# Second-stage expert products over 408 instead of 416 slots, in an order planned anew

## The chip, the cores and the metric

The kernel runs on one core of a Trainium2 chip. The metric is the time of one execution on the device in microseconds (us); less is better. Engines are named as in the profile: PE is TensorE's matmul, PEld its weight load, DVE is VectorE, ACT is ScalarE, POOL is GpSimd and SP is SyncE, which here only issues DMAs.

## The reference, cut to what matters

Three layers follow each other on 1536 tokens of 512 numbers. The first is attention in which a query sees only keys of the same hash bucket. The second is a mixture of 8 experts in which each token goes to one expert. The third is the one that the change touches most: each token goes to the two best of 8 experts.

```python
def _moe2_ref(x, w_gate, w_noise, noise, w1, w2):
    logits = x @ w_gate
    noisy_logits = logits + np.log1p(np.exp(x @ w_noise)) * noise
    top2 = np.argpartition(-noisy_logits, 2, axis=1)[:, :2]
    ...
    for e in range(E):
        for k in range(2):
            mask = top2[:, k] == e
            h = np.maximum(x[mask] @ w1[e], 0.0)
            out[mask] += top2_w[mask, k, None] * (h @ w2[e])
```

On the drawn inputs the second mixture sends 386, 404, 368, 376, 389, 374, 397 and 378 tokens to its experts (counted from the reference).

## The kernel before

**Stages.** Attention and the routing of the first mixture are one planned phase. Both mixtures together are the second phase. In it an expert is called a key: keys 0 to 7 are the first mixture's experts, keys 8 to 15 the second's. A token's row is scattered to its expert's slots in DRAM (`xs1`, `xs2`), and an expert's rows are read back from there. An expert of the second mixture has `CAP2` = 416 slots; a token beyond that is counted by `run_over`, and a count over zero runs a slow fallback over all tokens.

**One expert.** `x_turn`, `x_h` and `x_l` turn its rows and split each number into a high and a low half in a reduced float type. `mm1` forms the first product in four pairs of pieces, `relu_h` and `relu_l` apply the ReLU and split again, `mm2` forms the second product in eight pieces (blocks d = 0 to 3, halves p = 0 and 1). A piece is 12 matmuls: three products (high-high, low-high, high-low) for each 128 rows of the contraction. The moving operand has one column for each slot, so its width is `cap`. Weights come in chunks of 512 KB, eight for an expert, issued by SP into a ring of four raw buffers; ACT copies the high half (`wsplit_h`) and DVE subtracts the low one (`wsplit_l`).

**After the product.** For keys 8 to 14, ACT copies a finished block from PSUM to `YS` (`y_copy`), DVE turns it in 32 x 32 blocks (`y2_turn`, 13 blocks of 32 slots, so it reads all 416 columns) and weights it (`y2_weight`), and POOL adds it to the output in 13 scatters (`y2_add`). There is one buffer `yo` for the turned rows, so a key's first turn waits until the scatters of the key before have landed. Key 15 is different: its rows are gathered from the output (`y2_gather`), added on chip, and written by four scatters (`y2_put`), in four blocks of `MB` = 104 slots. Three blocks go through `mm2` (312 columns) and transposes, the fourth is formed row by row in two halves (`mm2_rows`, 256 columns). Key 8 is special at its start: part of its rows is read back in four blocks of `MB` rows and transposed by PE, and `y_put` adds the rows of the last first-mixture expert straight into PSUM.

**What sets the order.** Every engine works its instructions in the order in which they were emitted. A planner (`Plan.order`) decides that before the kernel is built. Each step has an engine, an assumed length in ns, the steps that it needs, the buffers that it holds, and a due time in us. The planner goes through time with these lengths. At each choice it takes, among the steps that could start within a short look-ahead (`WAITS`, `WAITS2`: a fixed time or a share of the step's length), the one with the earliest due time. `LENGTH` and `LENGTH2` replace assumed lengths by others; a pair is a length and a landing delay after it. `SHIFT` and `SHIFT2` add to the due times of groups of steps. In the second phase a group is a step's kind and a letter: a for keys 0 to 5, b for 6 to 8, c for 9 to 14, d for 15. `m1` and `m2` are the pieces of the two products, with due times `z + 2.1 * (2 * fp + f)` and `z + 2.1 * (8 + 2 * d + p)` for keys 8 to 15, where z is 37 us later for each key. The step `wr` stands for a weight chunk's transfer.

Of the kernel before, what the change touches and what calls it, by code (L numbers as in the profile page):

```python
# [13 lines left out]
AF = mybir.ActivationFunctionType  # L14
# [7 lines left out]
N, D, E, F = NB * S, NHEAD * DH, 8, 1024  # L22
NT = N // 128
CAP1 = 224
PB = CAP1 // 2
CAP2 = 416
MB = CAP2 // 4
NQ = CAP2 // 32
RW1 = D + 2 + E
RW2 = D + 1 + E  # L30
# [28 lines left out]
WAITS = {'PE': (0, 0.0), 'ACT': (95, 0.2), 'DVE': (35, 0.53), 'POOL': (1120, 0.0)}  # L59
LENGTH2 = {('POOL', 'gm', 1742): 2363, ('POOL', 'iw', 1100): 750, ('ACT', 'wh', 520): 521, ('DVE', 'wl', 600): 602, ('Q', 'wr', 2100): (2100, 1500), ('POOL', 'xm', 1023): 783,  # L60
    ('ACT', 'xh', 241): 243, ('DVE', 'xlo', 303): 310, ('ACT', 'xh', 427): 470, ('DVE', 'xlo', 536): 533, ('PE', 'm1', 1336): 1340, ('ACT', 'rh', 425): 441,
# [5 lines left out]
    ('DVE', 'xm', 150): 105, ('PE', 'xt', 430): 224, ('ACT', 'xh', 400): 403, ('DVE', 'xlo', 503): 509, ('ACT', 'xh', 745): 791, ('DVE', 'xlo', 936): 933,  # L67
# [3 lines left out]
SHIFT2 = {'g1a': -170, 'g2a': -15, 'g2b6': -95, 'g4a': -35, 'g5a': 1.3, 'g5aa': -230, 'g8a': -15, 'g9a': 26, 'gia': 23,  # L71
    'gib6': -120, 'gpa': -15, 'm1a': -13, 'm1b': 16, 'm1d': 5, 'm2a': -8, 'm2b': 19, 'm2c': 8, 'rha': -45,
    'rhb': -170, 'rla': -25, 'rlb': 60, 'rlc': -65, 'rld': -65, 'sqa': -17, 'wh0a': -20, 'wh1a': -15, 'wh1b': -115,
    'wl0a': -33, 'wl0b': 60, 'wl0c': 35, 'wl0d': -120, 'wl1a': -18, 'wl1b': 78, 'wl1c': 20, 'wl1d': -60, 'wr0a': -15,
    'wr0b': -20, 'wr1a': -30, 'wr1b': -35, 'xla': -20, 'xlb': -125, 'xloa': -120, 'xlob': -85, 'xloc': 75, 'xmc': 50,
    'xmd': -120, 'xta': -20, 'xtc': -40, 'yc0b': -55, 'yca': -10, 'yra': -5, 'yta': -2, 'ywd': -15}
WAITS2 = {'PE': (120, 0.0), 'ACT': (120, 0.5), 'DVE': (0, 0.01), 'POOL': (120, 0.0)}
WAIT = 120
ROUTING = ("rsa", "rsb", "r7", "rm", "rr0", "rr", "rq", "rp", "rn", "rv", "re", "rg", "ra", "rc", "ro", "xa", "xb", "oh", "xo")
PR = dict(sc=-5.4, mx=-8.7, ex=-5.34, pv=3.37, fin=3.38, bits=-14.64, prep=-18.57, load=-37.69, h=-17.66, l=0)  # L80
# [11 lines left out]
LATE, ZP, Z2, L6, CR = 1, 21.9, 205.0, -4, 12  # L92
# [88 lines left out]
def lsh_attention_moe_moe2_kernel(  # L181
# [144 lines left out]
    def run_over(pool, pi, i8, cap, K, T, dst, va=None, n=128):  # L326

        g = nc.gpsimd
        p = pool.tile([n, 2, K, T], F32, name="ov")
        g.tensor_copy(p[:, 0], pi)  # L330
        g.tensor_copy(p[:, 1], i8[:, :, 0:K].rearrange("p t k -> p k t"))
        g.tensor_scalar(p[:, 1], p[:, 1], float(N), float(cap), op0=OP.mult, op1=OP.add)
        g.tensor_tensor(p[:, 0], p[:, 0], p[:, 1], op=OP.subtract)
        if va is None:
            g.tensor_scalar(dst, p[:, 0], 0.0, None, op0=OP.is_ge)
        else:
            g.tensor_scalar(p[:, 1], p[:, 0], 0.0, None, op0=OP.is_ge)
            g.tensor_tensor(dst, p[:, 1], va[:, None, :].to_broadcast([n, K, T]), op=OP.mult)
# [854 lines left out]
    def y_copy(key, cap, d):  # L1193
        YS[key, d] = yp.tile([128, CAP2], F32, name="ys", bufs=6)
        o = cap if halves(key, d) else 0
        nc.scalar.activation(YS[key, d][:, :cap], Y[key, d][:, o:o + cap], AF.Copy)

    def y_add(key, cap, d):
        nc.vector.tensor_tensor(YS[key, d][:, :cap], Y[key, d][:, :cap], YS[key, d][:, :cap], op=OP.add)
# [65 lines left out]
    def y_put(dp, b):  # L1265
        for k in range(2):
            for d in range(2):
                x = ROWS[b, dp][k][:, d * 128:d * 128 + 128]
                nc.tensor.matmul(XP[E, 2 * dp + d][:, :CAP2], x, ONES[0][:, b], start=False, stop=b + k == 2)

    def r2_rank0(e):
        R2[e]["R"] = psp.tile([128, 512], F32, name="O", bufs=1)
# [14 lines left out]
        scat2.append(s)  # L1287

    def r2_over(e):
        run_over(r2, R2[e]["pi"], R2[e]["i8"], CAP2, 2, 2,  # L1290
                 rmax[:PB, NT + 4 * e:NT + 4 * e + 4].rearrange("p (k t) -> p k t", k=2), VA[e], PB)


# [12 lines left out]
    def x2_load(e):  # L1306
        if e:
            x2_rest(e)
            X2[e] = x_load(xs2, e, CAP2)
        else:  # L1310
            X2[0] = xin.tile([128, 4 * D], F32, name="xr")[:, :4 * D].rearrange("p (b c) -> p b c", c=D)
            nc.sync.dma_start(X2[0][:MB], xs2[0:CAP2].rearrange("(b p) c -> p b c", p=MB)[:, :, :D])

    def x2_rest(e):
        x = XM[8 + e] = yp.tile([128, NQ, RW2 - D], F32, name="xm2", bufs=3)
        if e < E - 1:
            for a in range(4):
                nc.sync.dma_start(x[32 * a:32 * a + 32], xs2[e * N:e * N + CAP2].rearrange("(b j) c -> j b c", j=32)[:, :, D:])
        else:
            nc.sync.dma_start(x[:MB, :4], xs2[e * N:e * N + CAP2].rearrange("(b p) c -> p b c", p=MB)[:, :, D:])  # L1320

    def x2_meta(e):
        if e < E - 1:
# [104 lines left out]
            add(("wl", n, k), "DVE", 600, P(wsplit_l, n, 2, k), z + k + .5, [("wh", n, k)] + ([("xlo", 0, 2)] if (n, k) == (4, 0) else []),  # L1428
                use=([("raw", n)] if n >= 8 else []) + [("w%d" % (c // 4), n)])
    for key in range(2 * E):  # L1430
        z, cap, one = Z[key], CAP1 if key < E else CAP2, key < E
        e = key % E
        q = 1.236 if one else 2.1
        if one:
# [32 lines left out]
        for fp in range(4):  # L1467
            for f in range(2):
                o = z + q * (2 * fp + f)
                add(("m1", key, fp, f), "PE", 1336 if one else 2276, P(mm1, key, cap, fp, f), o,  # L1470
                    [("xlo", key, i) for i in range(1 if fp + f == 0 else len(xp))]
                    + [("wl", key * 8 + fp, 0 if fp + f == 0 else 1)] * (key > 0)
                    + ([("m1", key, fp, 0)] if f else []),
                    use=[("w0", key * 8 + fp)] + [("x", (key, i)) for i in range(len(xp))]
                    + ([("S", ("m", key, fp))] if f else []), new=[] if f else [("S", ("m", key, fp))])
            o = z + q * (2 * fp + 2)
            add(("rh", key, fp), "ACT", 425 if one else 745, P(relu_h, key, cap, fp), o - CR, [("m1", key, fp, 1)],
                use=[("S", ("m", key, fp))], new=[("hh", (key, fp))])
            add(("rl", key, fp), "DVE", 535 if one else 936, P(relu_l, key, cap, fp), o - CR, [("rh", key, fp)],
                use=[("S", ("m", key, fp)), ("hh", (key, fp))])  # L1480
        yk = lambda d: ("S", "y72") if (key, d) == (E - 1, 2) else ("ET", ("y", key, d))
        for d in range(4):
            for p in range(2):
                o = z + q * (8 + 2 * d + p)
                c2 = 3 * MB if key == 2 * E - 1 else cap
                add(("m2", key, d, p), "PE", 1258 if one else 12 * int(c2 * .452 + 2), P(mm2, key, c2, d, p), o,
                    [("rl", key, 2 * p), ("rl", key, 2 * p + 1)]
                    + [("wl", key * 8 + 4 + d // 2 * 2 + p, 1)]
                    + ([("m2", key, d, 0)] if p else []),
                    use=[("w1", key * 8 + 4 + d // 2 * 2 + p)]  # L1490
                    + [("hh", (key, c)) for c in range(2 * p, 2 * p + 2)] + ([yk(d)] if p else []),
                    new=[] if p else [yk(d)])
            o = z + q * (10 + 2 * d)
            add(("yc0" if halves(key, d) else "yc", key, d), "ACT", 238 if one else 398, P(y_copy, key, c2, d), o - CR, [("m2", key, d, 1)],
                use=[yk(d)], new=[("ys", (key, d))])
            if halves(key, d):
                add(("yc", key, d), "DVE", 300, P(y_add, key, c2, d), o - CR, [("yc0", key, d)], use=[yk(d), ("ys", (key, d))])
# [225 lines left out]
```

## Time and profile before

| | us |
|---|---|
| median of 3 runs | 765.57 |
| lowest, highest | 765.16, 767.86 |
| the profiled execution's own time | 765.78 |
| its span, first to last instruction | 764.0 |
| TensorE busy in the span | 748.8 |
| VectorE, ScalarE, GpSimd busy | 569.5, 471.1, 390.8 |

The profiled execution is 1.78 us longer than its span and 0.2 us over the median. Attention fills the first 260 us or so, the first mixture lasts until about 460 us, and the second until 756 us, when TensorE's last matmul begins. A matmul's duration in the trace is longer than the distance to the next one's start, since they are pipelined; what a matmul costs in a row of them is read from the starts.

### The profile page before, as it was taken

To read this page: it belongs to the slowest core of one execution; us is meant where nothing else is said; L and a number is where in the kernel's file an instruction comes from. 1 tells how busy PE (TensorE), PEld (TensorE's weight loads), DVE (VectorE), ACT (ScalarE), POOL (GpSimd) and SP (SyncE) were. 2 spreads that over 40 slices of the span, in tenths; PEclk is the share of its full clock that TensorE was granted. 3 is DMA by queue.
4 is the path that set the end of the run, shared out by engine and by line. 5 is a ranking of instruction groups with operands and counts; after the bars stand their busy time and mean duration, and the time that the engine had idled before them with its cause. 6 is when DMAs were issued, how large, how long until landed. Compare 5 with 4: busy or idle time off the path is not lost. (4 is left out here: it accounts for less than half of the span.)

```text
span 764.0 us, 14517 instructions
## 1 busy us (share of the span) xinstructions
PE 748.8 (98%) x4851; PEld 726.9 (95%) x4851; DVE 569.5 (75%) x1249; ACT 471.1 (62%) x1009; POOL 390.8 (51%) x666
## 2 busy tenths in 40 slices
PE   8999999999999999999999999999999999999995
PEld 7999999999989999999999989999999999999995
DVE  7989989999989858988888766675757575754411
ACT  7889899898878747656566646453445344444210
POOL 6543445566666530445334443028564664748574
PEclk9999999999999999999999999999999999999999
DMA  7778886987774478777678586949797694946143
GB/s 193 190 202 229 213 221 176 274 212 184 161 186 147 151 199 266 215 236 251 194 212 253 178 238 173 222 149 239 142 222 172 137 225 104 218 120 121 18 36 84
DMA packets 142114, 140.61 MB, mean 184 GB/s; under 512 B 25898, under 2 KB 122434, under 8 KB 142034
## 3 DMA queue, kind: packets, MB, share of 16 engines
q1 hardware_dynamic: 124770, 122.93, 58.5%
q0 software_dynamic: 17264, 16.69, 11.5%
q8 instruction: 40, 0.66, 0.4%
q14 instruction: 40, 0.33, 0.1%
HBM read 88.54 MB, written 34.46 MB: 161 GB/s over the span
## 5 line engine op out<-in xcount | busy, mean ns | idle before, releaser
L1359 POOL DMA_INDIRECT out_dram<-yo,idx x91 | 149.6, 1644 | 125.0 <-DVE yo L1356 99.3
L1136 PE MATMUL S<-xh,w0h 128*128 128x224 f32 (+1 forms) x512 | 162.2, 317 | 0.5 <-DVE hh L1149 0.4
L1138 PE MATMUL S<-xh,w0l 128*128 128x224 f32 (+1 forms) x512 | 160.5, 313 | 0.0
L1137 PE MATMUL S<-xl,w0h 128*128 128x224 f32 (+1 forms) x512 | 159.8, 312 | 0.0
L273 DVE TENSOR_TENSOR w1l<-wraw,w1h 128x512 fp32r<-128x512 f32 x128 | 82.8, 684 | 35.9 <-ACT w1h L267 35.6
L693 DVE TENSOR_TENSOR el<-ET,eh 128x384 fp32r<-128x384 f32 x192 | 99.0, 549 | 6.4 <-ACT eh L687 4.9
L1145 ACT ACTIVATE hh<-S 128x448 fp32r<-128x448 f32 (+1 forms) x64 | 45.0, 703 | 93.8 <-PE S L1138 92.2
L687 ACT ACTIVATE eh<-ET 128x384 fp32r<-128x384 f32 x192 | 91.0, 496 | 16.9 <-PE ET L683 16.4
L675 ACT ACTIVATE es<-S,mxs 128x768 f32<-128x768 f32 x96 | 95.9, 999 | 8.2 <-POOL mxs L671 6.2
L665 DVE TENSOR_REDUCE mxs<-S 128x1 f32<-128x768 f32 x96 | 91.6, 954 | 12.3 <-PE S L660 9.3
L1137 PEld LDWEIGHTS S<-xl,w0h 128*128 128x128 f32 x512 | 97.1, 190 | 1.4 <-DVE xl L1122 0.5
L1136 PEld LDWEIGHTS S<-xh,w0h 128*128 128x128 f32 x512 | 97.1, 190 | 1.1 <-DVE hh L1149 0.6
L1138 PEld LDWEIGHTS S<-xh,w0l 128*128 128x128 f32 x512 | 97.2, 190 | 0.4
L267 ACT ACTIVATE w1h<-wraw 128x512 fp32r<-128x512 f32 x128 | 73.2, 624 | 34.6 <-PE ET L1172 27.1
L1149 DVE SCALAR_TENSOR_TENSOR hh<-S,hh 128x448 fp32r<-128x448 f32 (+1 forms) x64 | 52.5, 820 | 52.7 <-ACT hh L1145 52.5
L1172 PE MATMUL ET<-hh,w1h 128*128 128x416 f32 (+2 forms) x264 | 90.2, 342 | 1.1 <-DVE hh L1149 1.1
L1173 PE MATMUL ET<-hh,w1l 128*128 128x416 f32 (+2 forms) x264 | 91.0, 345 | 0.0
L683 PE MATMUL ET<-idf,es 128*128 128x128 f32 x576 | 90.0, 274 | 1.0 <-DVE el L693 1.0
L1171 PE MATMUL ET<-hh,w1h 128*128 128x416 f32 (+2 forms) x264 | 90.4, 343 | 0.0
L267 ACT ACTIVATE w0h<-wraw 128x512 fp32r<-128x512 f32 (+1 forms) x152 | 78.1, 560 | 8.2 <-DMA wraw<-in_w1b_dram 7.1
L273 DVE TENSOR_TENSOR w0l<-wraw,w0h 128x512 fp32r<-128x512 f32 x120 | 77.4, 685 | 7.7 <-ACT w0h L267 7.6
L683 PEld LDWEIGHTS ET<-idf,es 128*128 128x128 f32 x576 | 71.0, 142 | 8.8 <-DVE el L693 1.5
(270 smaller groups left out, 1605.5 us busy)
## 6 DMA issues: line engine op xcount, KB each, us to landing
wraw<-in_w1a_dram SPq DMA_DIRECT2D x32, 512.0 KB, 5.4
wraw<-in_w2a_dram SPq DMA_DIRECT2D x32, 512.0 KB, 4.9
wraw<-in_w1b_dram SPq DMA_DIRECT2D x32, 512.0 KB, 4.4
wraw<-in_w2b_dram SPq DMA_DIRECT2D x32, 512.0 KB, 4.3
xs<-zrow SPq DMA_DIRECT2D x26, 260.5 KB, 4.1
xr<-xs SPq DMA_DIRECT2D x28, 208.0 KB, 4.9
qk<-in_qk_dram SPq DMA_DIRECT2D x15, 384.0 KB, 4.1
xs<-zrow SPq DMA_DIRECT2D x14, 261.0 KB, 3.8
```

The source lines that it names most:

```text
L267: nc.scalar.activation(wH[n][:, c], wraw[n][:, c], AF.Copy)
L273: eng.tensor_tensor(wL[n][:, c], wraw[n][:, c], wH[n][:, c], op=OP.subtract)
L665: nc.vector.tensor_reduce(MX[(3 * g + j) % 9][:, 0:1], SC[g, j][:, :, :384], axis=AX.XY, op=OP.max, negate=True)
L675: nc.scalar.activation(ES[g, j].rearrange("p (a b) -> p a b", a=2), SC[g, j][:, :, :384], AF.Exp, bias=mx[:, 2:3], scale=mx[:, 1:2], accum ...
L683: nc.tensor.transpose(T[:, j * 128:j * 128 + 128], ES[g, j][:, kb * 128:kb * 128 + 128], idf)
L687: nc.scalar.activation(EH[g, kb], ET[g, kb], AF.Copy)
L693: nc.vector.tensor_tensor(EL[g, kb], ET[g, kb], EH[g, kb], op=OP.subtract)
L1136: nc.tensor.matmul(o, wH[n][:, fs], xh, start=kd == 0, stop=False)
L1137: nc.tensor.matmul(o, wH[n][:, fs], xl, start=False, stop=False)
L1138: nc.tensor.matmul(o, wL[n][:, fs], xh, start=False, stop=kd == 3)
L1173: nc.tensor.matmul(P, wL[n][:, ws], hh, start=False, stop=f == 7)
L1359: s = nc.gpsimd.indirect_dma_start(out=out.rearrange("n (a c) -> (n a) c", a=4), out_offset=bass.IndirectOffsetOnAxis(ap=IDX[e][:, b:b + 1 ...
```

## The change

The products of keys 8 to 15 use 408 columns instead of 416. `MB` becomes 102, so key 15's three blocks have 306 columns, and key 8's blocks have 102 rows. Reads of whole experts from `xs2` stay at 416 rows. Since DVE still turns 416 columns of `YS`, one more ACT instruction for each block of keys 8 to 14 fills the last 8 with ones. The overflow count uses 408. In the planner, the override for `wr` is gone, so a weight chunk's landing delay is the step's own 1300 ns instead of 1500. The assumed lengths of the products follow the width, the copy with the filler is longer, and the shifts and look-aheads of the second phase are all other numbers; a look-ahead of the first phase changes in its third digit. So the order of the second phase's instructions changes on every engine.

```diff
+USE2 = 408
-MB = CAP2 // 4
+MB = USE2 // 4
...
-WAITS = {'PE': (0, 0.0), 'ACT': (95, 0.2), 'DVE': (35, 0.53), 'POOL': (1120, 0.0)}
+WAITS = {'PE': (0, 0), 'ACT': (95, 0.2), 'DVE': (35, 0.5337189177802887), 'POOL': (1120, 0)}
...
-LENGTH2 = {('POOL', 'gm', 1742): 2363, ('POOL', 'iw', 1100): 750, ('ACT', 'wh', 520): 521, ('DVE', 'wl', 600): 602, ('Q', 'wr', 2100): (2100, 1500), ('POOL', 'xm', 1023): 783,
+LENGTH2 = {('POOL', 'gm', 1742): 2363, ('POOL', 'iw', 1100): 750, ('ACT', 'wh', 520): 521, ('DVE', 'wl', 600): 602, ('POOL', 'xm', 1023): 783, ('ACT', 'xh', 241): 243,
...
-    ('PE', 'm1', 2276): 2267, ('ACT', 'rh', 745): 761, ('DVE', 'rl', 936): 941, ('PE', 'm2', 2280): 2267, ('ACT', 'yc', 398): 414, ('DVE', 'yt', 502): 528,
+    ('PE', 'm1', 2232): 2222,
+    ('ACT', 'rh', 745): 761, ('DVE', 'rl', 936): 941, ('PE', 'm2', 2232): 2222, ('ACT', 'yc', 598): 640, ('DVE', 'yt', 502): 528, ('DVE', 'yw', 730): 743,
...
-SHIFT2 = {'g1a': -170, 'g2a': -15, 'g2b6': -95, 'g4a': -35, 'g5a': 1.3, 'g5aa': -230, 'g8a': -15, 'g9a': 26, 'gia': 23,
-    'gib6': -120, 'gpa': -15, 'm1a': -13, 'm1b': 16, 'm1d': 5, 'm2a': -8, 'm2b': 19, 'm2c': 8, 'rha': -45,
...
+SHIFT2 = {'g1a': -220, 'g2a': -90, 'g2b6': -90, 'g3a': -80, 'g5a': -10, 'g5aa': -255, 'g8a': 2, 'g9a': 20, 'gca': -100,
+    'gia': 15, 'm1a': -6.7, 'm1b': 15, 'm1c': 18, 'm1d': 25, 'm2a': -10, 'm2b': 15, 'm2c': 25, 'm2d': 140,
...
-WAITS2 = {'PE': (120, 0.0), 'ACT': (120, 0.5), 'DVE': (0, 0.01), 'POOL': (120, 0.0)}
+WAITS2 = {'PE': (85, 0), 'ACT': (120, 0.8), 'DVE': (120, 0), 'POOL': (775, 0)}
...
         nc.scalar.activation(YS[key, d][:, :cap], Y[key, d][:, o:o + cap], AF.Copy)
+        if E <= key < 2 * E - 1:
+            nc.scalar.activation(YS[key, d][:, cap:], ones[:, :CAP2 - cap], AF.Copy)
...
-                nc.tensor.matmul(XP[E, 2 * dp + d][:, :CAP2], x, ONES[0][:, b], start=False, stop=b + k == 2)
+                nc.tensor.matmul(XP[E, 2 * dp + d][:, :USE2], x, ONES[0][:, b, :USE2], start=False, stop=b + k == 2)
...
-        run_over(r2, R2[e]["pi"], R2[e]["i8"], CAP2, 2, 2,
+        run_over(r2, R2[e]["pi"], R2[e]["i8"], USE2, 2, 2,
...
-            nc.sync.dma_start(X2[0][:MB], xs2[0:CAP2].rearrange("(b p) c -> p b c", p=MB)[:, :, :D])
+            nc.sync.dma_start(X2[0][:MB], xs2[0:USE2].rearrange("(b p) c -> p b c", p=MB)[:, :, :D])
...
-        z, cap, one = Z[key], CAP1 if key < E else CAP2, key < E
+        z, cap, one = Z[key], CAP1 if key < E else USE2, key < E
```

## Rows read from the trace of the kernel before

**Rows 1.** The page's first part: span; busy us, share and count of TensorE.

```profile
span 764.0 us, 14517 instructions
PE 748.8 (98%) x4851; PEld 726.9 (95%) x4851; DVE 569.5 (75%) x1249; ACT 471.1 (62%) x1009; POOL 390.8 (51%) x666
```

**Rows 2.** Waits of PE, 430 to 764 us: total us, times, longest.

```profile
PE ET L1172 <- DVE hh L1149: 1.1, 1, 1.1
PE S L807 <- DMA xr<-xs: 0.6, 1, 0.6
PE ET L1220 <- ACT ys L1196: 0.4, 1, 0.4
```

**Rows 3.** Stretches: length; busy PE, PEld, DVE, ACT, POOL; PEclk; DMA share; GB/s.

```profile
480.00:500.00 20.00, 18.92 (x101) 18.39 (x100) 13.65 (x24) 8.03 (x14) 0.00 (x0) 1.00 0.98 243
500.00:520.00 20.00, 20.00 (x108) 19.82 (x107) 16.81 (x26) 12.77 (x22) 7.51 (x4) 1.00 0.54 157
```

**Rows 4.** Timeline of PE, 699 to 752 us: start, duration, line, tiles, shape.

```profile
699.12 0.35 PE L1171 MATMUL ET<-hh,w1h 128*128 128x416 f32 x1
...
716.68 0.35 PE L1171 MATMUL ET<-hh,w1h 128*128 128x416 f32 x1
...
737.12 0.30 PE L1171 MATMUL ET<-hh,w1h 128*128 128x312 f32 x1
...
748.58 0.30 PE L1171 MATMUL ET<-hh,w1h 128*128 128x312 f32 x1
...
749.00 0.28 PE L1183 MATMUL ET<-w1h,hh 128*104 128x256 f32 x1
...
751.48 0.28 PE L1183 MATMUL ET<-w1h,hh 128*104 128x256 f32 x1
```

**Rows 5.** Timeline of POOL, 719 to 764 us; in brackets idle before and its end.

```profile
719.75 1.75 POOL L1359 DMA_INDIRECT out_dram<-yo,idx  x1 [6.32 <-DVE yo L1356]
...
742.20 1.55 POOL L1359 DMA_INDIRECT out_dram<-yo,idx  x1 [0.30 <-issue]
...
757.80 1.00 POOL L1369 DMA_INDIRECT out_dram<-yo,idx  x1 [0.30 <-issue]
```

**Rows 6.** Timeline of DVE, 714 to 757 us.

```profile
714.79 1.60 DVE L1351 STREAM_TRANSPOSE yo<-ys 128x416 f32<-128x416 f32 x3 [4.04 <-DMA out_dram<-yo,idx]
...
718.00 0.61 DVE L1351 STREAM_TRANSPOSE yo<-ys 128x416 f32<-128x416 f32 x1 [0.44 <-ACT ys L1196]
...
738.21 1.02 DVE L1149 SCALAR_TENSOR_TENSOR hh<-S,hh 128x832 fp32r<-128x832 f32 x1 [5.25 <-ACT hh L1145]
752.11 0.48 DVE L1190 SCALAR_TENSOR_TENSOR yo<-ET,wc,xr 104x256 f32<-104x256 f32 x1 [12.87 <-DMA xr<-out_dram,idx]
...
756.18 0.48 DVE L1190 SCALAR_TENSOR_TENSOR yo<-ET,wc,xr 104x256 f32<-104x256 f32 x1 [0.24 <-PE ET L1185]
```

**Rows 7.** Groups of PE by line and shape, whole span: count; busy, mean ns.

```profile
L1136 PE MATMUL S<-xh,w0h 128*128 128x416 f32 x256 | 89.8, 351 | 0.0
L1171 PE MATMUL ET<-hh,w1h 128*128 128x416 f32 x224 | 78.5, 350 | 0.0
```

**Rows 8.** Groups of ACT by line and shape, 440 to 764 us.

```profile
L1145 ACT ACTIVATE hh<-S 128x832 fp32r<-128x832 f32 x32 | 27.7, 866 | 68.3 <-PE S L1138 67.9 <-PE ET L1173 0.3
...
L384 ACT ACTIVATE sp<-lg 112x16 f32<-112x16 f32 x1 | 0.2, 216 | 0.4 <-DVE lg L1241 0.4
```

**Rows 9.** Timeline of PE, 567 to 573 us: starts of pieces at key 10's end.

```profile
567.71 0.35 PE L1136 MATMUL S<-xh,w0h 128*128 128x416 f32 x1
...
569.97 0.35 PE L1171 MATMUL ET<-hh,w1h 128*128 128x416 f32 x1
...
572.24 0.35 PE L1136 MATMUL S<-xh,w0h 128*128 128x416 f32 x1
```

**Rows 10.** Waits of ACT, 480 to 764 us: total us, times, longest.

```profile
ACT w0h L267 <- DMA wraw<-in_w1b_dram: 7.1, 2, 3.6
```

**Rows 11.** Line L1171: weight loads, duration min/median/max in ns, all three widths.

```profile
L1171 PEld LDWEIGHTS ET<-hh,w1h x264: 187/188/192, 448.1 to 748.4; 128*128 128x128 f32 x132
```

More of the change, by code (lines that the diff above doesn't have):

```diff
@@ L58 @@
     'xb6': 60}
-WAITS = {'PE': (0, 0.0), 'ACT': (95, 0.2), 'DVE': (35, 0.53), 'POOL': (1120, 0.0)}
-LENGTH2 = {('POOL', 'gm', 1742): 2363, ('POOL', 'iw', 1100): 750, ('ACT', 'wh', 520): 521, ('DVE', 'wl', 600): 602, ('Q', 'wr', 2100): (2100, 1500), ('POOL', 'xm', 1023): 783,
-    ('ACT', 'xh', 241): 243, ('DVE', 'xlo', 303): 310, ('ACT', 'xh', 427): 470, ('DVE', 'xlo', 536): 533, ('PE', 'm1', 1336): 1340, ('ACT', 'rh', 425): 441,
[5 rows of a table removed]
-    ('DVE', 'xm', 150): 105, ('PE', 'xt', 430): 224, ('ACT', 'xh', 400): 403, ('DVE', 'xlo', 503): 509, ('ACT', 'xh', 745): 791, ('DVE', 'xlo', 936): 933,
[3 rows of a table removed]
@@ L71 @@
-SHIFT2 = {'g1a': -170, 'g2a': -15, 'g2b6': -95, 'g4a': -35, 'g5a': 1.3, 'g5aa': -230, 'g8a': -15, 'g9a': 26, 'gia': 23,
-    'gib6': -120, 'gpa': -15, 'm1a': -13, 'm1b': 16, 'm1d': 5, 'm2a': -8, 'm2b': 19, 'm2c': 8, 'rha': -45,
[L73 to L76, printed above, removed]
@@ L77 @@
-WAITS2 = {'PE': (120, 0.0), 'ACT': (120, 0.5), 'DVE': (0, 0.01), 'POOL': (120, 0.0)}
+WAITS = {'PE': (0, 0), 'ACT': (95, 0.2), 'DVE': (35, 0.5337189177802887), 'POOL': (1120, 0)}
+LENGTH2 = {('POOL', 'gm', 1742): 2363, ('POOL', 'iw', 1100): 750, ('ACT', 'wh', 520): 521, ('DVE', 'wl', 600): 602, ('POOL', 'xm', 1023): 783, ('ACT', 'xh', 241): 243,
[10 rows of a table added]
+SHIFT2 = {'g1a': -220, 'g2a': -90, 'g2b6': -90, 'g3a': -80, 'g5a': -10, 'g5aa': -255, 'g8a': 2, 'g9a': 20, 'gca': -100,
+    'gia': 15, 'm1a': -6.7, 'm1b': 15, 'm1c': 18, 'm1d': 25, 'm2a': -10, 'm2b': 15, 'm2c': 25, 'm2d': 140,
+    'rha': -15, 'rhb': -160, 'rhc': -40, 'rhd': -120, 'rla': -20, 'rlb': 45, 'sqa': -17, 'wh0a': -29, 'wh0b': -31,
+    'wh1a': -22.1, 'wh1b': -110, 'wl0a': -45, 'wl0b': 55, 'wl0d': -85, 'wl1a': -12, 'wl1b': 65, 'wl1c': 30, 'wr0a': -25,
+    'wr0b': -20, 'wr1a': -130, 'wr1b': -70, 'wr1c': 170, 'xha': -35, 'xhb': -15, 'xhc': 80, 'xla': -20, 'xlb': -165,
+    'xloa': -40, 'xloc': 80, 'xtb': 50, 'xtc': -15, 'yc0a': -195, 'yca': -40, 'ycc': 50, 'yra': -19, 'yta': -1}
@@ L1319, in x2_rest @@
         else:
-            nc.sync.dma_start(x[:MB, :4], xs2[e * N:e * N + CAP2].rearrange("(b p) c -> p b c", p=MB)[:, :, D:])
+            nc.sync.dma_start(x[:MB, :4], xs2[e * N:e * N + USE2].rearrange("(b p) c -> p b c", p=MB)[:, :, D:])
     def x2_meta(e):
@@ L1469, in lsh_attention_moe_moe2_kernel @@
                 o = z + q * (2 * fp + f)
-                add(("m1", key, fp, f), "PE", 1336 if one else 2276, P(mm1, key, cap, fp, f), o,
+                add(("m1", key, fp, f), "PE", 1336 if one else 2232, P(mm1, key, cap, fp, f), o,
                     [("xlo", key, i) for i in range(1 if fp + f == 0 else len(xp))]
@@ L1493, in lsh_attention_moe_moe2_kernel @@
             o = z + q * (10 + 2 * d)
-            add(("yc0" if halves(key, d) else "yc", key, d), "ACT", 238 if one else 398, P(y_copy, key, c2, d), o - CR, [("m2", key, d, 1)],
+            add(("yc0" if halves(key, d) else "yc", key, d), "ACT", 238 if one else 398 if key == 2 * E - 1 else 598, P(y_copy, key, c2, d), o - CR, [("m2", key, d, 1)],
                 use=[yk(d)], new=[("ys", (key, d))])
```

14 rows, old and new, of the table LENGTH2 are left out of this document.

## Prediction

> **What bounds the kernel now.** I read the page's first part first: TensorE is busy for 748.8 of 764.0 us and no other engine comes near it [rows 1]. A busy TensorE can still hide waits, so the next view is who TensorE waited for from 430 us on, where the second stage lies: three waits, 1.1 + 0.6 + 0.4 = 2.1 us [rows 2]. By stretches, 480 to 500 us lacks 1.08 us (18.92 of 20), and the twelve stretches from 500 to 740 us all show 20.00 of 20 (the first stands), at a granted clock of 1.00, the upper of the two levels [rows 3]. So in the second stage the end moves with whatever TensorE's instructions cost, up to the tail.
>
> The tail has another limit. Key 14 is the last expert whose rows are scattered in 13 accumulating pieces. Its last three matmuls begin at 716.68 [rows 4]. Then ScalarE copies the last block, VectorE turns and weights it, and GpSimd issues 13 scatters from 719.75 to 742.20, four gathers, and four writes of which the last starts at 757.80 [rows 5]. VectorE's last half block starts at 756.18 and takes 0.48, so its write could have gone out about 0.3 us later, near 757.0; it went out at 757.80, behind the earlier writes [rows 5, 6]. So the end hangs on the GpSimd chain that starts with the end of key 14; key 15's products have some 0.8 us of slack against it.
>
> **Part 1, 408 columns.** What is a column worth? The starts of successive matmuls tell it. At 416 columns, 93 steps take 716.68 - 699.12 = 17.56 us, 188.8 ns each; at 312 columns, 81 steps take 11.46 us, 141.5 ns; at 256 columns, 21 steps take 2.48 us, 118.1 ns [rows 4]. The slope is 47.3/104 = 0.455 ns a column between 312 and 416, and 23.4/56 = 0.418 between 256 and 312. No row shows 408 columns. I take the nearer slope, 8 x 0.455 = 3.64 ns a matmul; the flatter one gives 3.34. A cost that goes in steps of 32 or 16 columns would give nothing, but 312 is a multiple of neither, and charged as 320 it would lie off the line (0.37 ns a column below it, 0.49 above), so I give that little weight.
>
> The Trainium skill, "TensorE: Matmul & The Clock Gate", section "Back-to-back issue gap", gives an isolated spacing of N/2.4 + 2.5 ns, that is 175.8 ns at 416 columns, where the row shows 188.8: the trace disagrees on the level and, at 0.417 ns a column, nearly agrees with the flatter slope. By that rule part 1 below would be 4.48 us, not 4.89.
>
> How many matmuls count: 96 in the first product and 96 in the second per expert (256 of one of the three lines over 8 experts, 224 of one of the other three over 7) [rows 7]. Keys 8 to 14 are ahead of the tail's chain: 7 x 192 = 1344 matmuls, 1344 x 3.64 = 4.89 us (4.49 by the flatter slope). The 16 matmuls that add the last first-stage expert's rows give 0.06. Key 15 saves 96 x 3.64 + 96 x 6 x 0.455 = 0.61 us, but of its own slack; its only hold on the chain is the first half block, at 752.11 just after TensorE's block that began at 749.00 and ahead of the first write [rows 4, 6]. I count 0.25 us for that, bounds 0 and 0.6. MB = 102 changes transposes by two columns: below 0.02 us.
>
> The elementwise work on 408 columns is some 15 ns shorter each on engines that wait for TensorE anyway: nothing. Loads of x stay 416 rows; the copies that VectorE turns stay 416 wide. The fullest expert has 404 tokens, so the overflow count stays zero.
>
> **Part 2, the filler.** 28 more ScalarE instructions write 8 columns of ones behind the copied 408. The nearest row is a 16-column ACTIVATE, 216 ns [rows 8]. That is 4 x 0.21 = 0.8 us per expert of 36 us, hidden beside TensorE: of 20 us ScalarE is busy 8.03 and 12.77 in the two stretches shown [rows 3]. Behind it in ScalarE's queue stand a weight split or a ReLU, 0.2 us later. On the path it stands once: between key 14's last copy and its last turn, +0.2 us (0 to 0.3). There VectorE had idled 0.44 us for that copy, so the turn is late by all of it [rows 6]. If key 14 came closer behind key 13, the turn of its first blocks would wait for key 13's scatters to land (the 4.04 us wait at 714.79), and only those 0.44 us would be left to gain; part 3 opens that up.
>
> **Part 3, the order.** Priorities can be worked out by hand from the shifts. In keys 9 to 13 the last piece of the second product was due at Z + 2.1 x 15 + 8 = Z + 39.5, and the next expert's first-product pieces at Z + 37, 39.1, 41.2: two go in between. The trace shows just that: first-product pieces at 567.71 and 572.24 with a second-product piece at 569.97 between [rows 9]. With the new shifts it is Z + 56.5 against Z + 55 and 57.1: only one in between. So each of keys 9 to 13 ends its second product about 12 x 0.19 = 2.3 us earlier, its scatters start and land earlier, and key 14's turn is no longer held. For key 14 itself the margin grows from 2.5 to 5.5, so nothing of key 15 gets ahead of it. TensorE's total is the same; moved pieces cost nothing as long as their weights are split in time. Before, the waits put 7.1 us on ScalarE for weights to land, in two waits of up to 3.6 [rows 10], and TensorE did not feel them.
>
> The landing delay falls from 1500 to 1300 ns in the planner only: splits may stand 0.2 us earlier in ScalarE's queue. If a chunk isn't there, ReLUs and copies behind it wait. I cost this at 0: two PSUM buffers hold 2 x 24 x 0.189 = 9.1 us of products, and a wait of 3.6 us was covered. Bounds for all of the order: a gain of 2.1 us (all waits of [rows 2] gone) to a loss of about 4 (a new stall like the 1.1 us one at three or four expert borders). The first phase's VectorE look-ahead goes from 0.53 to 0.5337 of a duration, some 4 ns on 1 us: 0, bounds 0.5 either way.
>
> **Sum.** 4.89 + 0.06 + 0.25 - 0.2 = 5.0 us. The profiled execution took 765.78 us (764.0 of span and 1.78 around it), so 760.8; the median of the runs shown is 0.2 lower, so **760.6 us**, 0.65% less.
>
> **Rivals.** *The order gives more*: the waits of [rows 2] go as well and the last write follows TensorE, 5.0 + 2.1 = 7.1 us less, 758.5. For it: the second product of key 8 is now due before key 9's first (Z + 46.5 against Z + 55), so its scatters start earlier; against: the 1.1 us wait was VectorE's, and nothing in the shifts aims at it.
>
> *The order gives some back*: one to four stalls of about 1.1 us in 260 to 500 us, where every first-stage shift changes and the DMA engines are 0.98 busy (480 to 500) [rows 2, 3]. 761.8 to 765, within 0.5%.
>
> *Slower*: late weights. ScalarE, and after it VectorE, works in order; a split placed ahead of a ReLU holds the ReLU until the chunk lands. A first-product piece pair takes 24 x 0.189 = 4.53 us; with the ReLU's 0.87 and its remainder's 1.02 behind a 3.6 us wait [rows 6, 8, 10], 5.5 us pass, and TensorE stands about 1.0 us when the other buffer is full too. It decides at a wait of about 2.6 us. One is harmless; to be slower by over 0.5% it must eat 5.0 + 3.8 = 8.8 us, one to two such stalls at each of 7 borders: about 770. Against it: 500 to 740 us shows no stall at all now, with such waits in it.
>
> *It does nothing*: the weight loads bound TensorE, not the columns. They are busy 19.82 of 20 us [rows 3] and each takes 188 ns, just the spacing at 416 columns. The Trainium skill, "Perfetto Trace Analysis", section "Identifying the Most-Contended Engine", takes LDWEIGHTS' busy share as the measure of how near TensorE is to its limit, which would read as full; by that rule the time stays. Against it: the loads are as long (187 to 192 ns) where matmuls are 141.5 ns apart [rows 4, 11], so they overlap. Then only order matters, 765.6.
>
> **Chances.** Forecast (759 to 761.7) 0.57; more 0.10; some back 0.22; does nothing 0.04; slower 0.07. Half a per cent, 3.8 us, is about what a measurement here can tell from no change. Faster: 0.57 + 0.10 = 0.67; same: 0.22 + 0.04 = 0.26; slower 0.07. The range takes in the forecast, the better half of "more" and nearly all of "some back": 758.0 to 765.0.
>
> **What would show it.** Matmuls of 408 columns about 185.2 ns apart (188.8: no column effect); keys 9 to 13 with one first-product piece of the next key, not two, before their last second-product piece; 13 scatters of key 14 starting about 4.7 us earlier, near 715.0, and the last write near 752.8; TensorE's waits after 430 us no more than 2.1 us. New waits on hh or weights between 260 and 500 us would be the order's price, and would make me wrong on the size; TensorE waits at most borders, on the sign.

## The result, and the profile after

The changed kernel takes 771.13 us, the median of runs from 770.76 to 772.17; the kernel before, beside it, 765.83. The ratio is 1.0065 with a 95% interval of 1.0049 to 1.0082: **slower by 0.65%**, where 0.65% faster was forecast. The profiled execution took 772.17 us with a span of 770.4, 6.4 us more than in [rows 1].

The page's first part and then TensorE's longest waits over the whole span (columns as in [rows 1] and [rows 2]):

```profile
span 770.4 us, 14536 instructions
PE 746.1 (97%) x4851; PEld 726.7 (94%) x4851; DVE 570.2 (74%) x1249; ACT 473.4 (61%) x1037; POOL 393.8 (51%) x666
...
PE S L808 <- DMA xr<-xs: 6.4, 1, 6.4
...
PE ET L1167 <- DVE hh L1150: 1.1, 1, 1.1
```

TensorE is busy for 2.7 us less than before and yet ends later. What is new is the first line of the waits. The wait of the transposes for key 8's x was 0.6 us in [rows 2] (L807 there) and is 6.4 us now. The 1.1 us wait for hh that [rows 2] shows at key 8's second product is gone; the one on L1167 lies in the first mixture, at 296.56 us, and the kernel before has none there.

The load and its first user, on the queue of SyncE and on TensorE, first in the kernel before:

```profile
447.71 0.35 SPq L1312 DMA_DIRECT2D xr<-xs  x1
...
454.75 2.03 PE L807 MATMUL S<-idf,xr 104*128 104x104 f32 x16 [0.63 <-DMA xr<-xs]
```

and in the kernel after, with key 8's first product behind them:

```profile
448.82 0.30 SPq L1315 DMA_DIRECT2D xr<-xs  x1
...
461.44 3.74 PE L808 MATMUL S<-idf,xr 102*128 102x102 f32 x16 [6.41 <-DMA xr<-xs]
...
473.18 0.35 PE L1137 MATMUL S<-xh,w0h 128*128 128x408 f32 x1
```

From its issue to its first use the load took 454.75 - 447.71 = 7.0 us; now it takes 461.44 - 448.82 = 12.6 us, for 102 partitions in place of 104. And a second cost follows it: the same 16 transposes take 3.74 us in place of 2.03. The stretches around it (columns as in [rows 3]) show why, one of before and four of after:

```profile
454.00:460.00 6.00, 5.37 (x45) 5.27 (x44) 4.95 (x24) 1.34 (x5) 1.71 (x3) 1.00 1.02 318
```

```profile
455.00:461.00 6.00, 0.03 (x1) 0.00 (x0) 3.21 (x16) 1.26 (x4) 1.45 (x2) 0.77 1.11 191
461.00:467.00 6.00, 5.56 (x26) 5.56 (x27) 0.71 (x2) 0.00 (x0) 0.00 (x0) 0.50 0.45 147
467.00:473.00 6.00, 6.00 (x26) 5.91 (x26) 1.34 (x8) 0.92 (x2) 3.61 (x4) 0.59 0.31 93
473.00:479.00 6.00, 6.00 (x34) 5.83 (x32) 5.03 (x10) 4.61 (x9) 1.39 (x7) 1.00 0.45 134
```

TensorE stands still from 455 to 461 us; the granted clock falls to 0.50, the lower of its two levels (1.2 GHz), and is 1.00 throughout again only in the stretch from 473 on. From the first transpose at 461.44 to 473 TensorE is busy all the time, and the transposes take nearly twice as long as before.

Cut at four points that both traces have, the 6.4 us split up as follows.

| stretch | before | after | difference |
|---|---|---|---|
| start to issue of key 8's load | 447.71 | 448.82 | +1.11 |
| issue of the load to its first use | 7.04 | 12.62 | +5.58 |
| first use to key 8's first product | 6.91 | 11.74 | +4.83 |
| key 8's first product to key 14's first scatter | 258.09 | 250.84 | -7.25 |
| key 14's first scatter to the end | 44.22 | 46.35 | +2.13 |
| span | 763.97 | 770.37 | +6.40 |

So the gain that was forecast came, and more of it (7.25 us between key 8's first product and key 14's scatters); a load of two partitions fewer took 10.4 us ahead of it, and the tail took 2.1.

The tail on GpSimd, beside [rows 5]: key 14's first and last scatter, the second of key 15's gathers, the last write:

```profile
724.02 1.75 POOL L1362 DMA_INDIRECT out_dram<-yo,idx  x1 [8.05 <-DVE yo L1359]
...
746.47 1.55 POOL L1362 DMA_INDIRECT out_dram<-yo,idx  x1 [0.30 <-issue]
...
752.94 1.19 POOL L1336 DMA_INDIRECT xr<-out_dram,idx  x1 [0.30 <-issue]
...
763.22 1.09 POOL L1372 DMA_INDIRECT out_dram<-yo,idx  x1 [0.30 <-issue]
```

The scatters start at 724.02, where 715.0 was forecast. From the last write's start to the end of the span it is 770.37 - 763.22 = 7.2 us, against 763.97 - 757.80 = 6.2 before: these gathers and writes have 102 rows each now.

### The profile page after: what moved, and what is told of

It reads as the page before. It is cut to its first block, busy times and chain, and to the rows that moved or that the text cites. A ratio compares the mean times of both kernels' runs of the same rounds, so it can differ in the third digit from the quotient of the medians.

```text
span 770.4 us, 14536 instructions
## 1 busy us (share of the span) xinstructions
PE 746.1 (97%) x4851; PEld 726.7 (94%) x4851; DVE 570.2 (74%) x1249; ACT 473.4 (61%) x1037; POOL 393.8 (51%) x666
## 5 line engine op out<-in xcount | busy, mean ns | idle before, releaser
L1139 PE MATMUL S<-xh,w0l 128*128 128x224 f32 (+1 forms) x512 | 158.9, 310 | 0.0
L1173 PE MATMUL ET<-hh,w1h 128*128 128x408 f32 (+2 forms) x264 | 89.8, 340 | 0.0
L1174 PE MATMUL ET<-hh,w1l 128*128 128x408 f32 (+2 forms) x264 | 89.6, 339 | 0.0
L1172 PE MATMUL ET<-hh,w1h 128*128 128x408 f32 (+2 forms) x264 | 89.2, 338 | 0.0
L1197 ACT ACTIVATE ys<-ET 128x224 f32<-128x224 f32 (+2 forms) x63 | 26.9, 428 | 87.4 <-PE ET L1174 58.3
```

The costliest lines, as they stand in the source:

```text
L1139: nc.tensor.matmul(o, wL[n][:, fs], xh, start=False, stop=kd == 3)
L1173: nc.tensor.matmul(P, wH[n][:, ws], hl_, start=False, stop=False)
```

## The experiments

The theory after the result: the number 102 itself. MB is the partition count of key 8's load, of its transposes, and of key 15's gathers and writes, and a copy over 102 partitions may be spread over fewer DMA engines than one over 104. The rivals: the new order puts the load where other traffic delays it; the shorter products or the filler do it; the landing delay moves weights in its way.

**Undoing 102 for the load alone.** The changed kernel, with key 8's load and transposes on 104 partitions:

```diff
+M8 = CAP2 // 4
...
-        slot_start(XP[E, d], X2[0], range(2 * half, 2 * half + 2), MB, d, True)
+        slot_start(XP[E, d], X2[0], range(2 * half, 2 * half + 2), M8, d, True)
...
-            nc.sync.dma_start(X2[0][:MB], xs2[0:USE2].rearrange("(b p) c -> p b c", p=MB)[:, :, :D])
+            nc.sync.dma_start(X2[0][:M8], xs2[0:CAP2].rearrange("(b p) c -> p b c", p=M8)[:, :, :D])
```

> The changed kernel, but key 8's rows are read back in four blocks of 104 partitions instead of 102 (its transposes have 104 columns again); order and all else as changed. Theory A (the transfer over 102 partitions lands late): TensorE's 6.4 us wait for xr falls below 1 us, the granted clock stays at 1.00 there, 771.1 becomes 760 to 761.5. Theory B (the new order puts other transfers in its way): the wait stays at 5 to 7 us and the time at 771. By the Trainium skill, DMA: Bandwidth & Descriptors, section on why a DMA increments its semaphore by 16 and not by 1, a copy is split over the largest number of engines up to 16 that divides its slowest dimension: 13 for 104 partitions, 6 for 102.

Measured: 761.09 us against 765.88 before, ratio 0.9943 (0.9925 to 0.9962). The load's issue, TensorE's wait for it, and the stretch 460 to 480 us:

```profile
446.77 0.34 SPq L1316 DMA_DIRECT2D xr<-xs  x1
...
PE S L809 <- DMA xr<-xs: 0.4, 1, 0.4
...
460.00:480.00 20.00, 20.00 (x109) 19.70 (x109) 13.85 (x23) 12.10 (x21) 5.26 (x9) 1.00 0.73 169
```

The first transpose begins at 453.68, 6.9 us after the issue. The wait is 0.4, the clock 1.00. From 1.0065 to 0.9943 is 1.2%, 9.3 us, and 10.0 by the medians: with the same order, the same weights and the same 408 columns, the load's partition count turns the slower kernel into a faster one. That removes the rivals for the main loss.

**Undoing 102 in the tail too.** Key 15 also goes back to blocks of 104, with products of 416 and 312 columns; keys 8 to 14 stay at 408. The planned lengths are those of the change, so the order is the same.

```diff
-MB = USE2 // 4
+MB = CAP2 // 4
...
-        z, cap, one = Z[key], CAP1 if key < E else USE2, key < E
+        z, cap, one = Z[key], CAP1 if key < E else USE2 if key < 2 * E - 1 else CAP2, key < E
```

> As e1, and key 15 too keeps four blocks of 104 with 416 and 312 columns; keys 8 to 14 have 408 columns; order as changed. If the gathers and writes of 102 rows are what lengthened the tail (10.7 us behind TensorE's last matmul, before 8.1), it is 1.5 to 2.5 us faster than e1: 758 to 759.5, and gathers land about 3.8 us after their start again, not 4.9. If the tail's length has another cause, it is 0 to 0.6 us slower than e1, by key 15's eight more columns.

Measured: 758.35 us, ratio 0.991 (0.9893 to 0.9926), the fastest of all here: the span is 755.1 us, against 758.9 for the experiment above. Key 15's third gather, the sum on VectorE that waits for it, the last write, and then the packets and the median time from issue to landing of the four gathers, first with blocks of 102 (experiment above), then of 104:

```profile
742.21 1.15 POOL L1337 DMA_INDIRECT xr<-out_dram,idx  x1 [0.30 <-issue]
...
747.07 0.75 DVE L1351 SCALAR_TENSOR_TENSOR yo<-O,wc,xr 102x512 f32<-102x512 f32 x1 [0.47 <-DMA xr<-out_dram,idx]
...
751.16 1.09 POOL L1373 DMA_INDIRECT out_dram<-yo,idx  x1 [0.30 <-issue]
...
DMA packets 639, 0.80 MB, mean 91 GB/s; under 512 B 438, under 2 KB 438, under 8 KB 637
...
xr<-out_dram,idx POOLq DMA_INDIRECT x4, 4.8
```

```profile
741.61 1.07 POOL L1336 DMA_INDIRECT xr<-out_dram,idx  x1 [0.30 <-issue]
...
745.42 0.75 DVE L1350 SCALAR_TENSOR_TENSOR yo<-O,wc,xr 104x512 f32<-104x512 f32 x1 [0.37 <-DMA xr<-out_dram,idx]
...
749.36 1.00 POOL L1372 DMA_INDIRECT out_dram<-yo,idx  x1 [0.30 <-issue]
...
DMA packets 320, 0.78 MB, mean 100 GB/s; under 512 B 130, under 2 KB 130, under 8 KB 319
...
xr<-out_dram,idx POOLq DMA_INDIRECT x4, 3.7
```

From the gather to the sum that waits for it: 4.9 us with 102 rows, 3.8 with 104. From the last write to the span's end: 758.86 - 751.16 = 7.7 us and 755.08 - 749.36 = 5.7. So the tail pays for 102 twice. For almost the same bytes the gathers of 102 rows moved in twice the packets, 438 of them under 512 bytes in place of 130 (windows from the first gather to just before the first write's data, 739.0 to 747.8 and 738.5 to 746.3 us). That the smaller packets are what makes them late was not tried.

**102 put into the kernel before.** The same 104 partitions, loaded as 102 + 2 by two copies:

```diff
-            nc.sync.dma_start(X2[0][:MB], xs2[0:CAP2].rearrange("(b p) c -> p b c", p=MB)[:, :, :D])
+            src = xs2[0:CAP2].rearrange("(b p) c -> p b c", p=MB)[:, :, :D]
+            nc.sync.dma_start(X2[0][:102], src[:102])
+            nc.sync.dma_start(X2[0][102:MB], src[102:])
```

> The kernel before, with one edit: key 8's load of 104 partitions is issued as two, one of 102 partitions and one of 2. Same rows, same order. Theory A: TensorE waits 5 to 7 us for xr and its clock falls after it, 765.8 becomes 774 to 777. Theory B: the wait stays at 0.6 us and the time within 1 us of 765.8.

Measured: 777.27 us, ratio 1.016 (1.0143 to 1.0177).

```profile
446.68 0.30 SPq L1313 DMA_DIRECT2D xr<-xs  x1
...
459.81 3.71 PE L807 MATMUL S<-idf,xr 104*128 104x104 f32 x16 [6.77 <-DMA xr<-xs]
```

13.1 us from issue to first use, a wait of 6.8, and transposes at half speed, in the old order with 416 columns (774 to 777 us had been expected). The loss needs nothing else of the change; and the transposes here have 104 columns, so their 3.71 us is the clock and not the shape.

**96 in the kernel before**, as the control for the split into two copies (`src[:96]` and `src[96:]`):

> The kernel before, with key 8's load issued as 96 partitions and 8 partitions. Theory A, in the form that the divisor of the partition count sets the spread: the rows land no later than before, TensorE's 0.6 us wait stays or goes, 765.0 to 766. If any cut of the load in two costs time (a second issue, a second wait), it is slower as e3 is, by several us. Theory B: 765.8.

Measured: 766.50 us, ratio 1.0006 (0.9988 to 1.0024); 448.87 to 455.80, that is 6.9 us, and a wait of 0.9. Two copies cost nothing that can be measured, and 96 partitions land no sooner than 104.

**100 and 103 in the kernel before** (100 + 4 and 103 + 1), one run each. Divisors decide between "fewer partitions, more time" and "so many engines": 100 = 10 x 10 and 103 is a prime.

> The kernel before, key 8's load issued as 100 and 4 partitions. The load landed 7.0 us after its issue in one piece of 104 or cut at 96, and 13.1 us cut at 102. If any count near 104 that isn't a multiple of 8 is slow, the 100 land as late as the 102 did, 12 to 13 us, time 775 to 777. If the landing follows the largest divisor of the count up to 16 (10 engines with 10 partitions each, against 6 with 17 and 13 with 8), it lands after about 7 + 2 x 0.68 = 8.4 us, TensorE waits 1.5 to 2.5 us and the time is 767 to 769.

> The kernel before, key 8's load issued as 103 partitions and 1. Landing so far: 6.9 us (96 + 8), 7.0 (104), 8.9 (100 + 4), 13.1 (102 + 2). If the spread follows a divisor of the partition count, 103 is prime and all of it goes through one engine: by the 0.61 us for each partition on one engine between 10 and 17 (8.9 to 13.1), 13.1 + 86 x 0.61 = 66 us, TensorE waits 55 to 65 us and the time is 820 to 840. If only the share over the last whole group of 8 or 16 counts, 103 lands like 102, 12 to 14 us, and the time is 775 to 779.

Measured: 773.14 us with 100 and 802.25 with 103. Issue and TensorE's wait, then for 103 two stretches (columns as in [rows 3]):

```profile
449.29 0.32 SPq L1313 DMA_DIRECT2D xr<-xs  x1
...
PE S L807 <- DMA xr<-xs: 3.5, 1, 3.5
```

```profile
447.80 0.26 SPq L1313 DMA_DIRECT2D xr<-xs  x1
448.11 24.93 SPq L1314 DMA_DIRECT2D xr<-xs  x1
...
PE S L807 <- DMA xr<-xs: 32.8, 1, 32.8
...
461.00:467.00 6.00, 0.00 (x0) 0.00 (x0) 0.00 (x0) 0.00 (x0) 0.00 (x0) 0.50 0.07 25
...
485.00:491.00 6.00, 4.83 (x23) 4.86 (x24) 0.01 (x1) 0.00 (x0) 0.00 (x0) 0.50 0.30 98
```

In 461 to 467 every compute engine stands and the DMA share is 0.07, about 1/16 = 0.0625, at 25 GB/s: one of the core's 16 DMA engines carries the load alone. The load is 103 x 4 rows of 2048 bytes, 843,776 bytes; at 25 GB/s that is 33.8 us, most of the 38.4 seen. With all five counts side by side:

| partitions | largest divisor up to 16 | partitions per engine by it | issue to first use, us |
|---|---|---|---|
| 96 | 16 | 6 | 6.9 |
| 104 | 13 | 8 | 7.0 (6.9 and 7.2 in the first two experiments) |
| 100 | 10 | 10 | 8.9 |
| 102 | 6 | 17 | 13.1 (12.6 in the changed kernel) |
| 103 | 1 | 103 | 38.4 |

The time goes with the partitions per engine, not with the number of partitions. The Trainium skill, "DMA: Bandwidth & Descriptors", section "Why a DMA increments its semaphore by 16 and not by 1", states it: a copy is spread over the largest number of engines, at most 16, that divides its outermost dimension. The order of the five runs agrees, and so does the DMA share from 1.2 to 2.7 us after the load's issue (96, 104 and 100 partitions, then 102 in the changed kernel; columns as in [rows 3]):

```profile
450.07:451.57 1.50, 1.50 (x15) 1.50 (x14) 1.01 (x3) 1.25 (x3) 0.78 (x2) 1.00 0.85 246
448.91:450.41 1.50, 1.50 (x15) 1.50 (x14) 0.78 (x2) 1.50 (x4) 1.12 (x2) 1.00 0.67 194
450.49:451.99 1.50, 1.50 (x15) 1.46 (x13) 1.50 (x4) 0.49 (x1) 0.25 (x1) 1.00 0.52 157
450.02:451.52 1.50, 1.50 (x14) 1.50 (x14) 0.97 (x2) 1.41 (x4) 0.93 (x2) 1.00 0.31 87
```

0.85, 0.67, 0.52 and 0.31, divided by 16, 13, 10 and 6, are 0.05 each time; with 103 partitions the same stretch shows 0.04, and 461 to 467 us the 0.07 above. The times agree less well: 103 was expected at some 66 us by scaling from 102, and took 38.4. At the 25 GB/s of the single engine, 17 partitions of 8192 bytes would take an estimated 5.6 us and 8 partitions 2.6, far less than the 13.1 and 7.0 seen. In the other runs the weight chunks follow on SyncE's queue within 1 us of the load's issue, and the DMA share is 1.11 in 455 to 461 us of the changed kernel; with 103 the queue's next issue took 24.9 us, so no chunk was issued before 473.15. An engine that shares its time with the weight chunks would explain the difference; that is argued, not shown. With 100 the time lost was also above the 767 to 769 us that was expected, because the clock fell here as well (0.81 in 460 to 480 us).

**The clock's part.** The changed kernel with 33 instead of 5 filler matmuls ahead of key 8's transposes, which keep TensorE working while it waits; planned length and order unchanged:

```diff
-            add(("wx",), "PE", 250 * WX, P(x8_warm, WX), z - 13.5, [("yt", 7, 3)], new=[x8(0)])
+            add(("wx",), "PE", 250 * WX, P(x8_warm, 33), z - 13.5, [("yt", 7, 3)], new=[x8(0)])
```

> The changed kernel with 33 instead of 5 filler matmuls of 512 columns ahead of key 8's transposes, so that TensorE works while it waits for the rows (some 28 x 0.23 = 6.4 us more); order and planned lengths unchanged. If the 213 ns transposes and 340 ns matmuls behind the wait (before: 112 and 189) come from the clock having fallen in the idle time, they return to 112 and 185 ns, key 8's first product starts 4 to 5 us earlier and 771.1 becomes 766 to 767. If the shape of 102 rows makes them slow, nothing changes: 770.5 to 772.

Measured: 766.03 us, ratio 0.9998 (0.998 to 1.0017), with the load as late as in the changed kernel.

```profile
452.44 7.76 PE L1096 MATMUL S<-wt 128*128 128x512 f32 x33
...
460.17 2.01 PE L808 MATMUL S<-idf,xr 102*128 102x102 f32 x16
...
455.00:461.00 6.00, 6.00 (x32) 5.09 (x32) 2.23 (x14) 0.22 (x1) 0.78 (x2) 1.00 1.01 209
```

The transposes take 2.01 us again and the clock is 1.00 through the wait. From 1.0065 to 0.9998 is 0.67%, 5.1 us, beside the 4.83 of the table in the result. So of the 10.4 us about half is the wait and half the clock that the wait leaves behind.

**The change's two halves, with blocks of 104.** First the order alone: 416 columns, no filler, the planned lengths of the change.

```diff
-USE2 = 408
+USE2 = 416
...
-        if E <= key < 2 * E - 1:
-            nc.scalar.activation(YS[key, d][:, cap:], ones[:, :CAP2 - cap], AF.Copy)
```

> The changed kernel's order on every engine, with 416 columns, blocks of 104 and no filler: the order alone. If the order is worth nothing by itself: 765.0 to 766.5. In the changed kernel's trace the 1.1 us wait of key 8's second product is gone, and the first stage lost about 0.9 us; the two cancel. If the order is a part of why the changed kernel was slow: 767 to 770. If it is worth having: 763 to 764.5.

Measured: 764.84 us against 767.01, ratio 0.9971 (0.9957 to 0.9985), 2.2 us less. Then the columns alone: the kernel before, in its own order, with `USE2 = 408` for keys 8 to 14 and the filler.

> The order of the kernel before on every engine; only keys 8 to 14 have 408 columns, with the filler; blocks of key 8 and key 15 stay 104. In the changed kernel's trace the matmuls of 408 columns stand 184.7 ns apart, 4.1 less than the 188.8 at 416. If all of it reaches the end: 1344 x 4.1 = 5.5 us, less 0.2 for the filler, 760.5. If with the old order key 14's turn is held by key 13's scatters (only 0.44 us to gain there), 0.3 us less, 760.8; then e2's 758.4 says that the order gives about 2 us when the columns are fewer. If it is 758 to 759 like e2, the order gives nothing.

Measured: 763.03 us, ratio 0.9945 (0.9926 to 0.9964), 4.2 us less by the ratio. That is less than the 5.0 to 5.3 us that was expected, and the profiled execution shows where: between key 8's first product and key 14's scatters the columns save 5.2 us, but key 8's load is issued at 451.42, 3.7 us later than in the kernel before, in the same order; the runs do not say why. By the ratios the two halves give 6.4 us together, beside 6.9 for the second experiment: they add up within the intervals.

**The landing delay.** The best kernel, planned with the old delay of 1500 ns:

```diff
+('Q', 'wr', 2100): (2100, 1500),
```

> e2 (408 columns, blocks of 104, changed order) planned with a landing delay of 1500 instead of 1300 ns for weight chunks. If the delay matters only through small moves of splits: within 1 us of e2's 758.4. If 1300 was too little and splits wait in ScalarE's queue: 756 to 757. If the order was searched for 1300 and is upset by 1500: 760 or more.

Measured: 776.33 us, ratio 1.0118 (1.0091 to 1.0145). TensorE's longest wait and the stretch 460 to 480 us:

```profile
PE O L306 <- DVE hot L412: 10.0, 4, 6.5
...
460.00:480.00 20.00, 16.71 (x103) 16.08 (x103) 8.09 (x36) 5.41 (x15) 9.96 (x21) 0.83 0.75 208
```

The wait is in the routing work, not on weights: 200 ns in one planned length give another order altogether, and shifts that fit 1300 do not fit 1500. It says nothing of how long a chunk takes; it says that the planner's numbers stand or fall together.

## Why the prediction was wrong

*What bounds the kernel* was read rightly, and it held: with TensorE full from 500 us on, what its instructions saved came out at key 14's scatters. The reading also said "in the second stage the end moves with whatever TensorE's instructions cost", and left out what comes just ahead of that stage: key 8's load stood on the path with TensorE waiting for it, 0.6 us in [rows 2].

*Part 1, the columns*: right. From key 8's first product at 473.18 to key 15's first at 721.43, behind key 14's last, it is 248.25 us, over 1344 matmuls 184.7 ns each, where 185.2 was forecast and 188.8 stood in [rows 4]. The columns alone gained 4.2 us by the ratio and 5.2 us between key 8's first product and key 14's scatters (258.09 to 252.88), beside the forecast's 4.89 - 0.2.

*The step that failed* stands at the end of part 1: "MB = 102 changes transposes by two columns: below 0.02 us", with "Loads of x stay 416 rows" behind it. The second sentence is true of the other experts' loads only: the diff cuts key 8's to USE2, which is 102 partitions. The first counts MB as columns of a matmul, but the diff also has it as `X2[0][:MB]` and `p=MB`, the partitions of a copy, and key 15's gathers and writes use it too. So the step that put the cost of MB = 102 at nothing had no term for the transfers. The price was 10.4 us at the load (5.6 landing, 4.8 clock) and, by the first two experiments, some 2.7 to 3.8 us more in the tail (761.09 - 758.35 by the medians, 758.9 - 755.1 by the spans). Against terms of 5.0 us these set the sign. The prediction shows no row with a copy over 102 partitions, so this cost had to be bounded, not set to zero.

*Part 2, the filler*: right in size. The one on the path, between key 14's last copy and its last turn:

```profile
722.04 0.20 ACT L1199 ACTIVATE ys<-ones 128x8 f32<-128x8 f32 x1
...
722.27 0.61 DVE L1354 STREAM_TRANSPOSE yo<-ys 128x416 f32<-128x416 f32 x1 [1.03 <-ACT ys L1199]
```

*Part 3, the order*: its pieces came as worked out, its price did not. Key 10's end, beside [rows 9]:

```profile
577.56 0.34 PE L1137 MATMUL S<-xh,w0h 128*128 128x408 f32 x1
...
579.77 0.35 PE L1172 MATMUL ET<-hh,w1h 128*128 128x408 f32 x1
...
581.99 0.34 PE L1137 MATMUL S<-xh,w0h 128*128 128x408 f32 x1
```

The first of these begins a first-product piece of key 11, the second the last second-product piece of key 10, the third the rest of key 11: one piece goes in between, where there were two before (567.71 and 572.24 in [rows 9]). It was costed at 0 with a bound of 2.1 for a gain, and is worth 2.2 (0.9971): the 1.1 us stall on hh, which "nothing in the shifts aims at", is gone, and key 8's second product runs in one piece. Between key 8's first product and key 14's scatters the order alone gives 1.4 us (258.09 to 256.71).

*The landing delay* was costed at 0 as 0.2 us on a split. In the changed plan it did no harm that shows, but the reasoning did not hold: the other value in the same plan costs about 16 us (ratios 1.0118 and 0.991), by another order and not by 0.2 us.

*The tail.* "key 15's products have some 0.8 us of slack" and a chain that shortens with it held only for blocks of 104. With 102 the sums wait for gathers, and the last write begins at 763.22, where 752.8 was forecast.

*The rivals.* "Slower" had the size, about 770, by luck: its loss was to come from late weights, but no new wait for weights appears, and the mechanism was another. "The order gives more" is near what the kernel with blocks of 104 did (758.35 beside 765.88, where 758.5 was named), with the stall on hh gone but a wait of 0.9 us for key 8's x left. The rival that was missing is the plain one: a size that was trimmed is also the shape of a transfer. That the order "gives some back" and that the change "does nothing" both fall: 2.2 us gained, and 4.1 ns fewer per matmul while the weight loads stayed as long (187 to 192 ns on L1172, as in [rows 11]).

*What stays open*: the 1.1 us before the load's issue (the issue lay anywhere from 446.41 to 451.42 in the kernels here with either of the two orders, and the 1.1 us wait at 296.56 us is in no other trace of the changed order at that length: 0.3 in the order alone, none in the first two experiments); whether the small packets are why indirect copies of 102 rows land later; and the size of the 103 case.

## What to carry to other kernels

When a size is trimmed, list every place where it appears, and for each transfer ask what it does to the partition count: 102 in place of 104 was 2% fewer bytes and nearly twice the time, because 104 has the divisor 13 and 102 only 6; loading the old 104 partitions and computing on fewer columns kept all of the gain. A new wait of TensorE can cost more than its length: here 6.4 us of standing brought 4.8 us at the lower clock behind it, and filler matmuls gave those back. Planner numbers (lengths, delays, shifts) that fit each other are to be changed together, and a change of one of them is costed by the order that it gives, not by its own size: 200 ns in one length cost some 16 us here.

## What the runs showed of the hardware that was not expected

- A load over 102 partitions took 12.6 to 13.1 us where 104 took 6.9 to 7.2, 100 took 8.9, and 103 took 38.4, with 25 GB/s at a DMA share of 0.07, one engine of 16. The share from 1.2 to 2.7 us after the issue was 0.85 with 96 partitions, 0.67 with 104, 0.52 with 100, 0.31 with 102.
- Cutting the load in two cost nothing that shows: 96 + 8 partitions landed in 6.9 us, and the time was 766.50 us beside 765.88.
- After 6.4 us of waiting, the granted clock was 0.50 in 461 to 467 us and 0.59 in 467 to 473, with TensorE busy for 11.6 of these 12 us; it was 1.00 from 473 on.
- Four indirect gathers of 102 rows landed 4.8 us after their issue (median) in 637 packets of the software queue, 438 of them under 512 bytes; of 104 rows after 3.7 us in 319 packets, 130 under 512 bytes, for 0.78 and 0.77 MB.
- At 408 columns matmuls follow each other every 184.7 ns, near the line through 312 and 416 columns (185.2), so the width is not rounded up to 416 (188.8).
